# Transposing the last eight LayerNorm blocks on TensorE instead of by DMA, with new planner constants, in an attention and gMLP kernel

## The chip, the cores and the metric

One core of one Trainium2 chip runs the whole kernel in one launch. The metric is the device time in microseconds (us) of one execution; the median of three runs is given. A core has five engines that run side by side: TensorE (PE, with its weight loads shown as PEld), VectorE (DVE), ScalarE (ACT), GpSimd (POOL) and SyncE (SP), whose queue here issues every DMA.

## The reference, cut to what matters

```python
# S = 2048 tokens, D = 448, 16 heads of 28, W = 8 keys per query, 2 apart; Fh = 896
x  = A_x
h  = x + A(layernorm(x))          # A: sliding, dilated attention
h2 = h + B(layernorm(h))          # B: gMLP

def A(x):
    q, k, v = heads(x @ wqkv)
    # query s sees keys s, s-2, ..., s-14 (those >= 0)
    attn = softmax(where(mask, q . k * scale, -1e9))
    return concat_heads(attn @ v) @ wo

def B(x):
    z  = gelu(x @ w_in)
    z1 = z[..., :Fh]
    z2 = layernorm(z[..., Fh:])
    g  = w_sp @ z2 + b_sp         # w_sp is 2048 x 2048: mixes the tokens
    return (z1 * g) @ w_out
```

The neighbours are taken by a band matrix: scores of a query block against all keys of its reach are computed densely, `exp` is taken, and the result is multiplied by a 0/1 mask (band, and even distance).

## The kernel before, in words

The kernel isn't a nest of loops in the order of its work. It fills a graph with tasks (`G.add`, `dma`), and `Graph.schedule` then plans them: a task names the engines that may do it with a planned duration, what it reads and writes, the buffers it takes, and a rank `prio`. The planner steps through planned time. It looks for the engine that can start something first, takes among the tasks that could start there within a short window the one of lowest rank, and so fixes the order of each engine's instructions and, where there is a choice between VectorE and ScalarE, the engine. `Sched` puts in the semaphores, and each engine runs its list in order. The ranks are formulas over constants in the dictionary `P` (L133 to L135); `pos(m)` is m * 128 / 114, the attention block in which 128-token block m lies.

The stages, each as tasks of 128-token blocks m = 0 to 15 or attention blocks i = 0 to 17 of 114 queries:

- Load of x (L505), of all weights, and small setup on GpSimd. The attention mask `maskb` is made from GpSimd's band tables by five small VectorE steps (L492 to L496) with the rank `mc`. 24 matmuls on constants (L550) with the last rank fill TensorE while it is otherwise idle.
- LN1, `layernorm(m, 0, ...)`, rank `ln_s * pos(m) + ln_o`: statistics (L558, L560) on VectorE, the reciprocal root on GpSimd (`rstd_of`, L608, L610), normalising into a block of the ring `tring` of six (L563), and a copy of 64 pad columns (L567). Then the transpose into `xT`, which holds the features on the partitions. `xT` lies in the memory of `wsp0`, so the profile shows it as `wsp`; `wqk` and `wv` lie in `early`. For m < `nld` = 8 four TensorE transposes go to PSUM (L582) and VectorE or ScalarE copies them out (`copy_on`, L604 or L605). For m >= 8 four DMA transposes of 128 by 128 write `xT` directly (L590).
- `xU` is `xT` with its two partition halves exchanged, so that two matmuls of 64 rows can run side by side in the array. For m < `npt` = 8 copies on VectorE or ScalarE make it; for m >= 8 two DMAs per group of four blocks do (L600).
- Q and K, `qk_pair(tc, g, ...)`: for each group tc of 512 tokens four pairs of matmul chains (L619) and an eviction on ScalarE. It needs `xT` and `xU` of the four blocks of its group.
- Attention, `att_block(i)`: V (L627), scores (L660), `exp` in two parts (L669), mask product on VectorE (L676, rank `mk`), the weighted sum (L681), normalising (L686, L688), transpose back (L693).
- `y_block(m)`: output projection (L627), residual (L708), and LN2, `layernorm(m, 1, ...)`, whose transposes go to `xB` by DMA (L451); its exchanged copy `xS` is made by DMA too (L576).
- gMLP: z2 with its gelu (L743) and LayerNorm (L747 to L752), rank `z0 + zs * pos(m)`, its gelu placed behind the `exp` of attention block `zb`; z1 with its gelu (L769), rank from `z1`, behind the last `exp`. `load_wsp` fetches w_sp in four parts of 16 DMA transposes (L451) into `wsp0` (only once `xT` is dead) and `wsp1`. `g_tile(fc, tc)` is 16 matmuls of 512 columns (L777), the bias (L782) and the product with z1 (L785). `wout_block(m)` is the last projection (L795), the residual (L799) and the store (L801). The ranks of these lie between 60 and 100.

All DMAs stand in SyncE's one queue in the planned order, and a DMA whose data isn't ready holds up those behind it. A DMA transpose of LN1 is planned with 0.45 us of that queue (`P_TR_US`).

Of the kernel before, what the change touches and what calls it, by code (L numbers as in the profile page):

```python
# [15 lines left out]
NCH = 4  # L16
# [83 lines left out]
class Task:  # L100
# [3 lines left out]
    def __init__(self, idx, alts, fns, reads, writes, adds, allocs, prio, keep, table, mode, twos, dma_us):  # L104
# [22 lines left out]
WIN = {"pe": 0.15, "act": 0.05, "dve": 0.15, "pool": 0.05, "sp": 0.05}  # L127
DMA_US = 2.6
NSEM = 96
P_TR_US = 0.45  # L130


P = dict(ln_s=0.9, ln_o=-0.7, qk_s=2.2, qk_o=-11.38, qk_g=-2.74, v=14.25, ve=2.52, lg=-13.21, ex=-15.44, mk=-14.58, av=2.77,  # L133
         nm=0.59, ot=-4.62, y=12.08, ln2=5.39, z0=150.45, zs=-0.36, zb=13, kz2=2, z1=116.86, kl=1, kq=0, kz=5, switch=13.45,
         npt=8, nld=8, mc=25.81)  # L135


class Graph:
# [30 lines left out]
    def schedule(self):  # L169
# [14 lines left out]
        while ready:  # L184
# [37 lines left out]
            lim = first[eng] + WIN[eng]  # L222
            best = min((c for c in by_task.values() if c[3] == eng and c[0] <= lim), key=lambda c: (c[2].prio + (P["switch"] if c[3] == "pe" and c[2].mode != mode else 0.0), c[2].idx))
            s, e_at, t, eng, d = best
# [113 lines left out]
def bass_sequential_preLN__sliding_local_dilated__mixer_gmlp__prompt_kernel(  # L338
# [13 lines left out]
    G = Graph()  # L352

    with contextlib.ExitStack() as top:
        def sb(name, shape, dt):
            return top.enter_context(nc.sbuf_tensor(name, shape, dt))
# [3 lines left out]
        tring = sb("tring", [128, NTR, DP], BF16)  # L360
        xB = sb("xB", [128, NB, NCH, 128], BF16)
        xS = sb("xS", [128, NB, NCH, 128], BF16)
        ident = sb("ident", [128, 128], BF16)
# [35 lines left out]
        psb = psum[:].bitcast(BF16)  # L399
# [6 lines left out]
        r_ident, r_mask, r_bb, r_warm, r_ij, r_half, r_wout = [  # L406
            Res(n) for n in ("ident", "mask", "bb", "warm", "ij", "half", "w_out")]
# [17 lines left out]
        P_bank = Pool("bank", 8)  # L425
# [16 lines left out]
        def banks(b, i, n, p1=128):  # L442

            s = sorted(x.slot for x in b)
            return psum[:].rearrange("p (b c) -> p b c", c=512)[0:p1, s[i]:s[i + 1] + 1:s[i + 1] - s[i], 0:n]

        def dma(fn, kb, reads=(), writes=(), prio=0.0, after=(), adds=(), allocs=()):
            return G.add([("sp", 0.5)], [fn], reads, writes, adds=adds, allocs=allocs, prio=prio, after=after, dma_us=kb / 180.0)

        def dma_t(dst, src, us, reads=(), writes=(), prio=0.0, adds=()):  # L450
            return G.add([("sp", us)], [lambda e: e.dma_start(dst(), src(), transpose=True)], reads, writes, adds=adds, prio=prio)  # L451

        def pe_us(n, cols):
            return n * (cols / 2400.0 + 0.003)

        def act_us(n, sbuf=False):
            return (n + (190 if sbuf else 105)) / 1200.0

        def dve_us(n, rate=1.0):
            return (n / rate + 85) / 960.0  # L460
# [3 lines left out]
        def pos(m):  # L464
            return m * 128.0 / NQ
# [25 lines left out]
        for fn, rd, wr in (  # L491
# [5 lines left out]
        ):  # L497
            G.add([("dve", 0.28)], [fn], rd, wr, prio=P["mc"])

# [49 lines left out]
        for i in range(NWARM):  # L549
            G.add([("pe", 0.22 if i > 12 else 0.43)], [lambda e: e.matmul(bank(wb, 512), ident[:, :], warm)],  # L550
                  reads=[r_ident, r_warm], writes=[] if i else [wb], adds=[wb] if i else [], allocs=[] if i else [wb],
                  prio=900)

        def layernorm(m, i, prio):

            k = i * NB + m
            s = Buf(P_st)
            G.add([("dve", dve_us(D))], [lambda e: e.bn_stats(st[:, s.slot, 0:6], x_tm[:, m, :])],  # L558
                  [r_x[m]], [s], [s], prio=prio)
            G.add([("dve", 0.10)], [lambda e: e.bn_aggr(mv[:, k, :], st[:, s.slot, 0:6])], [s], [r_mv[k]], prio=prio)  # L560
            rstd_of(k, prio)
            t = Buf(P_tr)
            G.add([("dve", 0.32)], [lambda e: e.tensor_scalar(tring[:, t.slot, 0:D], x_tm[:, m, :], mv[:, k, 0:1],  # L563
                                                              rstd[:, k:k + 1], ALU.subtract, ALU.mult)],
                  [r_x[m], r_mv[k], r_rs[k]], [t], [t], prio=prio, after=tr_init)
            if not i:
                G.add([("dve", dve_us(64, 4)), ("pool", 0.25)], [lambda e: e.tensor_copy(tring[:, t.slot, D:], tring[:, t.slot, 384:D])],  # L567
                      [t], [t], prio=prio)
            xm = (xB[:, m, :, :] if i else xT[:, :, 128 * m:128 * m + 128])
            um = (None if i else xU[:, :, 128 * m:128 * m + 128])  # L570
            rm, ru = (r_xhT[m], r_xS[m]) if i else (r_xT[m], r_xU[m])
            if i:
                dma_t(lambda: xm, lambda: tring[:, t.slot, :], 1.3, [t], [rm], prio)
                if m % 2:
                    for dst, src in ((LO, HI), (HI, LO)):
                        dma(lambda e, dst=dst, src=src: e.dma_start(xS[dst, m - 1:m + 1, :, :], xB[src, m - 1:m + 1, :, :]), 131,  # L576
                            r_xhT[m - 1:m + 1], [], prio=prio, adds=r_xS[m - 1:m + 1])
                return
            if m < P["nld"]:
                b = Buf(P_bank)  # L580
                G.add([("pe", 0.27)], [
                    lambda e, c=c: e.transpose(psb[:, b.slot * 1024 + c * 128: b.slot * 1024 + c * 128 + 128],  # L582
                                               tring[:, t.slot, c * 128:(c + 1) * 128], ident[:, :]) for c in range(NCH)],
                    [t, r_ident], [b], [b], prio=prio)
                G.add([("act", act_us(512)), ("dve", dve_us(512, 2))], [
                    lambda e: copy_on(e, xm, psb[:, b.slot * 1024: b.slot * 1024 + 512].rearrange("p (c t) -> p c t", c=NCH))],
                    [b], [rm], prio=prio)
            else:
                for c in range(NCH):
                    G.add([("sp", P_TR_US)], [lambda e, c=c: e.dma_start(xm[:, c, :], tring[:, t.slot, 128 * c:128 * c + 128], transpose=True)],  # L590
                          [t], [], adds=[rm], prio=prio)
            if m < P["npt"]:
                for ps, po in ((LO, HI), (HI, LO)):
                    G.add([("dve", dve_us(384, 4)), ("act", act_us(384, True))], [
                        lambda e, ps=ps, po=po: copy_on(e, um[ps, 0:3, :], xm[po, 0:3, :])], [rm], [], adds=[ru], prio=prio)
            elif m % 4 == 3:
                cols = slice(128 * m - 384, 128 * m + 128)
                rms, rus = r_xT[m - 3:m + 1], r_xU[m - 3:m + 1]
                for dst, src in ((LO, HI), (HI, LO)):
                    dma(lambda e, dst=dst, src=src: e.dma_start(xU[dst, :, cols], xT[src, 0:3, cols]), 196, rms, [], prio=prio, adds=rus)  # L600

        def copy_on(e, dst, src):
            if hasattr(e, "activation"):
                return e.activation(dst, src, AF.Copy)  # L604
            return e.tensor_copy(dst, src)  # L605

        def rstd_of(k, prio):
            G.add([("pool", 0.24)], [lambda e: e.tensor_scalar(va[:, k:k + 1], mv[:, k, 1:2], EPS, None, ALU.add)],  # L608
                  [r_mv[k]], [r_va[k]], prio=prio - 20)
            G.add([("pool", 0.61)], [lambda e: e.tensor_tensor(rstd[:, k:k + 1], va[:, k:k + 1], mhalf[:, 0:1], ALU.pow)],  # L610
                  [r_va[k], r_half], [r_rs[k]], prio=prio - 20)
# [5 lines left out]
        def pair(b, ws, xs, n):  # L617

            return [lambda e, j=j, u=u: e.matmul(bank2(b, j, n), ws(j, (LO, HI)[j], u), xs(j, (LO, HI)[j], u), start=(u == 0),  # L619
                                                 stop=(u == 6), tile_position=(64 * j, 0)) for u in range(7) for j in range(2)]  # L620
# [5 lines left out]
        def full(b, ws, xs, n, m=128):  # L626
            return [lambda e, c=c: e.matmul(bank(b, n, 0, m), ws(ALL, c), xs(ALL, c), start=(c == 0), stop=(c == NCH - 1))  # L627
                    for c in range(NCH)]

        def pair_us(n):  # L630
            return pe_us(7, n)

        def qk_pair(tc, gg, prio):
# [3 lines left out]
            def src(j, ps, u):  # L637
                if u == 6 or u % 2 == j:
                    return xT[ps, u // 2, cols]
                return xU[ps, u // 2, cols]  # L640
            G.add([("pe", pair_us(512))], pair(b, lambda j, ps, u: wqk[ps, u, gg, :], src, 512),
                  r_wqk + r_xT[4 * tc:4 * tc + 4] + r_xU[4 * tc:4 * tc + 4], b, b, prio=prio, mode=1, twos=True, keep=P["kq"])
            G.add([("act", act_us(1024))],
                  [lambda e: copy_on(e, qk[:, :, gg, cols], banks(b, 0, 512))], b, [r_qT[tc][gg], r_kT[tc][gg]], prio=prio)

        def att_block(i):
            t0, nq, k0, nk = _att_geom(i)
            v, b = Buf(P_V), Buf(P_bank)
            G.add([("pe", pe_us(4, D))], full(b, lambda ps, c: xT[ps, c, k0:k0 + nk], lambda ps, c: wv[ps, c, :], D, nk),
                  r_xT[k0 // 128:(k0 + nk - 1) // 128 + 1] + r_stv, [b], [b, v], prio=i + P["v"], after=v_init)  # L650
            G.add([("act", act_us(D)), ("dve", dve_us(D))], [
# [82 lines left out]
        for m in range(NB):  # L734
            k = 2 * NB + m
            s = Buf(P_st)
            p = P["z0"] + P["zs"] * pos(m)
            zb = [Buf(P_bank), Buf(P_bank)]
# [4 lines left out]
                lambda e, zb=zb, m=m: e.activation(z2p[:, m, :].rearrange("p (b c) -> p b c", b=2), banks(zb, 0, D), AF.Gelu_apprx_tanh)],  # L743
# [124 lines left out]
```

## Time and profile before

| | |
|---|---|
| median of three runs | 284.14 us (284.07 to 284.81) |
| the profiled execution | 284.14 us, its span 282.4 us |
| TensorE (PE) busy | 246.5 us, 87% of the span |
| VectorE (DVE) busy | 155.7 us, 55% |
| ScalarE (ACT) busy | 100.8 us, 36% |
| GpSimd (POOL) busy | 49.9 us, 18% |
| mean granted TensorE clock | 0.958 |

The span runs from the first to the last instruction. A row of waits names the waiting engine and line, whom it waited for, the total in us, the number of times and the longest. A row of a timeline has the start, the length, the engine, line and operation, and the tiles. The chain that ended last is followed back from the last instruction through whatever released each step; "SPq" is SyncE's queue, "DMA" the transfer itself. Matmuls of one pair run at the same time, so their durations overlap.

### The profile page before, as it was taken

Reading aid. Unit: us, or ns where it says so; the run is one execution under the profiler, and the core shown is the slowest. Engines: PE = TensorE matmul, PEld = TensorE weight load, DVE = VectorE, ACT = ScalarE, POOL = GpSimd, SP = SyncE. Lnnn points to the kernel's source line nnn. Section 1 sums busy time; section 2 is a strip of 40 time slices with the busy share of each in tenths; the row PEclk is TensorE's granted clock in tenths of the full one; section 3 lists DMA queues with packets and bytes.
Section 4 is the critical chain, followed back from the end, with each engine's and each line's share of the span. In section 5 each row is a group of like instructions: output and inputs, shape, how many; then the busy total and the mean of one; then the engine's idle time right before and its main releaser. Section 6 shows DMA issues by size and latency. Waiting matters only on the chain.

```text
span 282.4 us, 5019 instructions
## 1 busy us (share of the span) xinstructions
PE 246.5 (87%) x2044; PEld 121.1 (43%) x2044; DVE 155.7 (55%) x354; ACT 100.8 (36%) x122; POOL 49.9 (18%) x125
## 2 busy tenths in 40 slices
PE   6996993049449999998799999999999999999994
PEld 2442462025215664544355444444444444444442
DVE  4968989204275899998798300753333333333333
ACT  2657787007409998996466600000000000000000
POOL 9442603200031021433443200000000000000000
PEclk9998899559959999999999999999999999999999
DMA  6990141131153405564555362444403442010001
GB/s 159 317 235 2 38 96 23 28 74 27 34 123 76 94 2 81 131 112 93 123 99 116 64 182 56 70 96 98 121 2 81 104 97 84 0 65 0 2 0 65
DMA packets 62806, 23.07 MB, mean 82 GB/s; under 512 B 53184, under 2 KB 61632, under 8 KB 62784
## 3 DMA queue, kind: packets, MB, share of 16 engines
q1 hardware_dynamic: 62784, 22.76, 35.5%
q8 instruction: 16, 0.26, 0.4%
q14 instruction: 6, 0.05, 0.1%
HBM read 6.49 MB, written 1.84 MB: 29 GB/s over the span
## 4 chain that ended last, share of the span: by engine, by line
PE 75%; DVE 8%; SPq 6%; DMA 3%; POOL 3%; ACT 2%; issue 2%; DVEq 0%; POOLq 0%
PE psum L777 34%; PE psum L619 22%; PE psum L795 7%; PE psum L627 7%; SPq L590 4%; DMA xU<-wsp 2%; PE psum L681 2%; SPq L451 2%; DVE z1p L676 2%; PE psum L660 1%; ACT z1p L669 1%; DVE st L747 1%; DVE tring L563 1%; DVE xU L605 1%; PE psum L693 1%
## 5 line engine op out<-in xcount | busy, mean ns | idle before, releaser
L782 DVE TENSOR_TENSOR qk<-psum,bb 128x512 bf16<-128x512 f32 x28 | 19.3, 690 | 68.8 <-PE psum L777 68.8
L777 PE MATMUL psum<-wsp,z2p 128*128 128x512 bf16 x224 | 48.9, 379 | 0.0
L777 PE MATMUL psum<-early,z2p 128*128 128x512 bf16 x224 | 48.8, 379 | 0.0
L619 PE MATMUL psum<-wsp,early 64*128 64x512 bf16 x128 | 29.3, 417 | 22.2 <-DMA xU<-wsp 22.2
L669 ACT ACTIVATE z1p<-psum 128x912 bf16<-128x912 f32 (+2 forms) x36 | 33.5, 934 | 1.7 <-PE psum L660 1.2
L604 ACT ACTIVATE qk<-psum 128x1024 bf16<-128x1024 f32 (+1 forms) x26 | 21.8, 841 | 33.4 <-PE psum L619 33.4
L777 PEld LDWEIGHTS psum<-wsp,z2p 128*128 128x128 bf16 x224 | 21.8, 98 | 26.6 <-issue 0.4
L777 PEld LDWEIGHTS psum<-early,z2p 128*128 128x128 bf16 x224 | 21.9, 98 | 26.3
L610 POOL TENSOR_TENSOR rstd<-va,mhalf 128x1 f32<-128x1 f32 x48 | 31.6, 658 | 3.7
L608 POOL TENSOR_SCALAR va<-mv 128x1 f32<-128x1 f32 x48 | 12.2, 254 | 95.6 <-DVE mv L560 77.2
L619 PE MATMUL psum<-xU,early 64*128 64x512 bf16 x96 | 27.1, 424 | 0.0
L619 PE MATMUL psum<-w,xB 64*128 64x448 bf16 x112 | 22.7, 350 | 2.8 <-DMA xS<-xB 1.5
L619 PEld LDWEIGHTS psum<-wsp,early 64*128 64x128 bf16 x128 | 11.3, 103 | 31.8 <-issue 25.2
L619 PE MATMUL psum<-w,xS 64*128 64x448 bf16 x112 | 22.7, 350 | 0.0
L795 PE MATMUL psum<-xS,z1p 128*128 128x448 bf16 x112 | 21.8, 353 | 0.0
L619 PE MATMUL psum<-xB,w 64*128 64x512 bf16 x98 | 21.8, 377 | 0.0
L619 PE MATMUL psum<-xS,w 64*128 64x512 bf16 x98 | 21.8, 377 | 0.0
L747 DVE BATCH_NORM_STATS2 st<-z2p 128x6 f32<-128x448 bf16 x32 | 19.4, 606 | 3.6 <-ACT z2p L743 3.3
L676 DVE TENSOR_TENSOR z1p<-z1p,maskb 128x1824 bf16<-128x1824 bf16 (+2 forms) x18 | 19.8, 1100 | 2.0 <-ACT z1p L669 1.8
L558 DVE BATCH_NORM_STATS2 st<-x_tm 128x6 f32<-128x448 bf16 x32 | 19.4, 605 | 1.6 <-DMA x_tm<-in_A_x_dram 1.5
L769 ACT ACTIVATE z1p<-psum 128x1024 bf16<-128x1024 f32 x14 | 14.3, 1023 | 8.5 <-PE psum L619 8.5
L563 DVE TENSOR_SCALAR tring<-x_tm,mv,rstd 128x448 bf16<-128x448 bf16 x32 | 12.3, 392 | 9.1 <-DMA xB<-tring 6.6
(69 smaller groups left out, 278.8 us busy)
## 6 DMA issues: line engine op xcount, KB each, us to landing
xS<-xB SPq DMA_DIRECT2D x16, 128.0 KB, 2.4
out_dram<-tring SPq DMA_DIRECT2D x16, 112.0 KB, 1.7
x_tm<-in_A_x_dram SPq DMA_DIRECT2D x1, 896.0 KB, 8.2
w<-in_B_w_in_dram SPq DMA_DIRECT2D x8, 112.0 KB, 3.3
early<-in_A_wqkv_dram SPq DMA_DIRECT2D x2, 392.0 KB, 5.5
w<-in_B_w_in_dram SPq DMA_DIRECT2D x2, 392.0 KB, 7.8
xS<-in_B_w_out_dram SPq DMA_DIRECT2D x1, 784.0 KB, 4.7
xU<-wsp SPq DMA_DIRECT2D x4, 192.0 KB, 2.9
```

Source lines behind the costliest of these rows:

```text
L558: G.add([("dve", dve_us(D))], [lambda e: e.bn_stats(st[:, s.slot, 0:6], x_tm[:, m, :])], [r_x[m]], [s], [s], prio=prio)
L563: G.add([("dve", 0.32)], [lambda e: e.tensor_scalar(tring[:, t.slot, 0:D], x_tm[:, m, :], mv[:, k, 0:1], rstd[:, k:k + 1], ALU.subtract, A ...
L604: return e.activation(dst, src, AF.Copy)
L610: G.add([("pool", 0.61)], [lambda e: e.tensor_tensor(rstd[:, k:k + 1], va[:, k:k + 1], mhalf[:, 0:1], ALU.pow)], [r_va[k], r_half], [r_rs[ ...
L619: return [lambda e, j=j, u=u: e.matmul(bank2(b, j, n), ws(j, (LO, HI)[j], u), xs(j, (LO, HI)[j], u), start=(u == 0), stop=(u == 6), tile_p ...
L627: return [lambda e, c=c: e.matmul(bank(b, n, 0, m), ws(ALL, c), xs(ALL, c), start=(c == 0), stop=(c == NCH - 1)) for c in range(NCH)]
L669: lambda e, hh=hh: e.activation(E[0:nk, ev.slot, hh * 4:hh * 4 + 8, 0:nq].rearrange("p (b g) q -> p b g q", b=2), banks(lb, hh, 512, nk).r ...
L676: lambda e: e.tensor_tensor(E[0:nk, ev.slot, :, 0:nq], E[0:nk, ev.slot, :, 0:nq], maskb[0:nk, mi:mi + 1, 0:nq].to_broadcast([nk, NHEAD, nq ...
L747: lambda e, h=h, m=m, s=s: e.bn_stats(st[:, s.slot, 6 * h:6 * h + 6], z2p[:, m, D * h:D * (h + 1)])],
L777: lambda e, s=s: e.matmul(bank(b, 512), z2p[:, s, fc * 128:(fc + 1) * 128], w[:, s, :], start=(s == 0), stop=(s == NB - 1)) for s in range ...
L782: G.add([("dve", dve_us(512))], [lambda e: e.tensor_tensor(ub[:, u.slot, :], bank(b, 512), bb[:, 512 * tc:512 * (tc + 1)], ALU.add)], [b, ...
L795: lambda e, f=f: e.matmul(bank(b, D), z1p[:, f, 128 * m:128 * m + 128], w_out[:, f, :], start=(f == 0), stop=(f == FC7 - 1)) for f in rang ...
```

## The change

LN1's path for blocks 8 to 15 becomes that of blocks 0 to 7: four TensorE transposes and one copy out of PSUM, in place of four DMA transposes. The constants `nld` and `P_TR_US` go. The exchange into `xU` for blocks 8 to 15 stays with the DMA. All the planner's constants in `P` but `kz2`, `kl` and `npt` get other values. The five mask steps and `wout_block` have the same text as before.

```diff
-P_TR_US = 0.45
...
-P = dict(ln_s=0.9, ln_o=-0.7, qk_s=2.2, qk_o=-11.38, qk_g=-2.74, v=14.25, ve=2.52, lg=-13.21, ex=-15.44, mk=-14.58, av=2.77,
-         nm=0.59, ot=-4.62, y=12.08, ln2=5.39, z0=150.45, zs=-0.36, zb=13, kz2=2, z1=116.86, kl=1, kq=0, kz=5, switch=13.45,
-         npt=8, nld=8, mc=25.81)
+P = dict(ln_s=0.13, ln_o=8.0, qk_s=2.85, qk_o=-21.56, qk_g=-2.68, v=11.96, ve=5.7, lg=-11.68, ex=-12.89, mk=-9.32, av=3.1,
+         nm=0.66, ot=-8.69, y=9.35, ln2=7.41, z0=63.24, zs=-1.6, zb=7, kz2=2, z1=109.63, kl=1, kq=1, kz=2, switch=7.46,
+         npt=8, mc=29.73)
...
-            if m < P["nld"]:
-                b = Buf(P_bank)
-                G.add([("pe", 0.27)], [
...
-            else:
-                for c in range(NCH):
-                    G.add([("sp", P_TR_US)], [lambda e, c=c: e.dma_start(xm[:, c, :], tring[:, t.slot, 128 * c:128 * c + 128], transpose=True)],
-                          [t], [], adds=[rm], prio=prio)
+            b = Buf(P_bank)
+            G.add([("pe", 0.27)], [
+                lambda e, c=c: e.transpose(psb[:, b.slot * 1024 + c * 128: b.slot * 1024 + c * 128 + 128],
+                                           tring[:, t.slot, c * 128:(c + 1) * 128], ident[:, :]) for c in range(NCH)],
+                [t, r_ident], [b], [b], prio=prio)
+            G.add([("act", act_us(512)), ("dve", dve_us(512, 2))], [
+                lambda e: copy_on(e, xm, psb[:, b.slot * 1024: b.slot * 1024 + 512].rearrange("p (c t) -> p c t", c=NCH))],
+                [b], [rm], prio=prio)
```

More of the change, by code (lines that the diff above doesn't have):

```diff
@@ L578, in layernorm @@
                 return
-            if m < P["nld"]:
-                b = Buf(P_bank)
-                G.add([("pe", 0.27)], [
[L582 to L587, printed above, removed]
-            else:
-                for c in range(NCH):
-                    G.add([("sp", P_TR_US)], [lambda e, c=c: e.dma_start(xm[:, c, :], tring[:, t.slot, 128 * c:128 * c + 128], transpose=True)],
-                          [t], [], adds=[rm], prio=prio)
+            b = Buf(P_bank)
[6 more added lines that the diff above has]
+                [b], [rm], prio=prio)
             if m < P["npt"]:
```

## The prediction

> **What bounds the kernel now.** I read the page's 40 slices first. In each row a digit is the busy tenths of a slice of 7.06 us.
>
> ```profile
> PE   6996993049449999998799999999999999999994
> DVE  4968989204275899998798300753333333333333
> PEclk9998899559959999999999999999999999999999
> ```
>
> TensorE is full from slice 20 (about 141 us) to the end. Before that there is a hole in slices 6 and 7 and a shallower one near slices 9 to 11, and VectorE is empty in the same places, so neither engine is the limit there. The waits say whom TensorE waits for (total us, times, longest):
>
> ```profile
> PE psum L619 <- DMA xU<-wsp: 22.2, 2, 14.3
> ```
>
> These are two waits of the Q/K projection (L619 in qk_pair) for the exchanged copy xU of tokens 1024 to 1535 and 1536 to 2047. The chain that ended last shows what stands before them (start, length, what):
>
> ```profile
> 53.27 1.23 SPq L590
> 54.55 1.23 SPq L590
> ...
> 56.33 0.63 SPq L600
> ...
> 57.02 2.91 DMA xU<-wsp
> 59.93 0.14 issue
> 60.06 6.62 PE psum L619 x42
> ...
> 160.86 24.28 PE psum L777 x112
> ```
>
> SyncE's queue issues one DMA transpose (L590) each 1.23 us, then the exchange (L600), and only then can TensorE go on. The same thing repeats up to 81.73. From 160.86 the chain is TensorE alone (L777, L795) to 278.73. The VectorE timeline shows that the data had long been there:
>
> ```profile
> 33.68 0.38 DVE L563 TENSOR_SCALAR tring<-x_tm,mv,rstd 128x448 bf16<-128x448 bf16 x1
> ...
> 49.05 0.39 DVE L563 TENSOR_SCALAR tring<-x_tm,mv,rstd 128x448 bf16<-128x448 bf16 x1
> ```
>
> Counting L563 and its pad copies L567 from the start, these are the normalised blocks 11 and 15, the last of the two groups. The exchanges start at 56.3 and 77.9, some 22 and 28 us later. That time is SyncE's queue.
>
> The windows answer prices the stages (PE busy, PEld, DVE, ACT, POOL, granted clock, DMA share, GB/s):
>
> ```profile
> 60.00:66.70 6.70, 6.64 (x50) 2.94 (x54) 0.00 (x0) 2.05 (x2) 0.00 (x0) 0.70 0.14 28
> 82.00:105.00 23.00, 22.90 (x322) 13.03 (x319) 18.28 (x37) 19.01 (x27) 4.60 (x11) 0.95 0.31 65
> 105.00:137.00 32.00, 28.96 (x352) 14.52 (x349) 29.25 (x67) 25.84 (x28) 10.10 (x24) 1.00 0.56 106
> ```
>
> After the hole the clock is 0.70, and three Q/K pairs take 6.62 us where a pair at full clock takes about 1.5 (four took 6.15 at 14.2). From 82 to 137 both TensorE and VectorE are nearly full.
>
> **The change part by part.** The diff holds two edits, the path of blocks 8 to 15 and the planner's constants. Nothing in it adds a mask step or alters wout_block, so I cost what the diff has.
>
> Removed: 32 DMA transposes at 1.23 us, 39.4 us of SyncE's queue between 27 and 76. Behind them now stand six loads of w1 (L530, held until 32.98), the exchanges L600 and the first LN2 transpose (L451 at 76.03), for which VectorE waited 6.6 us. The exchanges for blocks 8 to 15 stay: 0.6 us each to issue, 2.9 to land.
>
> Added: 8 times four TensorE transposes (L582). The chain has four at 0.34 to 0.40, so 2.7 us by the lower. Then 8 evictions of 128x512, 0.42 us on VectorE (3.4 in all) or 0.60 on ScalarE (4.8). TensorE is on the path, so its 2.7 counts in full. Evictions go to VectorE's sum below. New waits: TensorE's transposes stand in its order and can wait for a tring block; behind them wait projections and scores. The nearest row is TensorE waiting for L567 before L582, 2.0 us in three waits, 0.67 each: between 0 and 5.3 for eight. I take 0, since blocks 9 to 11 were ready within 3 us of each other.
>
> Where the stall goes: with block 11 normalised at 34.1, about 1 us for transpose and eviction and 3.5 us for the exchange, group 2 is ready near 39, before TensorE ran dry at 45.7. Group 3, from 49.5, is ready near 54. So both waits, 22.2 us, should go. Also the slow-clock stretches after them: 6.62 us against 4.6 for three pairs, and 4.52 against 3.1 for the two at 81.73, 3.5 us together.
>
> The Trainium skill speaks against this: "Advanced Engine Details and Errata", X-Bar Transpose (TRN2), says that transposing DMAs are as fast as plain ones, at 350 to 400 GB/s. As an estimate from that page, 32 transposes of 32 KB would take about 3 us of the queue, and the change would end near 281. The trace disagrees: a plain exchange of 192 KB holds the queue for 0.61 us, a transpose of 32 KB for 1.23, so the row decides.
>
> Sum against the profiled execution (284.14 us, span 282.4, 1.7 around it, equal to the median of the three runs): 284.14 - 22.2 - 3.5 + 2.7 = 261.1.
>
> What is late next is VectorE. It is busy 115.6 us before 160.86 (the ten-us windows added up); with the evictions, 119.0. The sum puts the spatial products (L777) at 160.86 - 23.0 = 137.9. From 82 to 137 VectorE was busy 47.5 of 55 us, 86%. At this pace from its first LayerNorm step at 2.9, 119.0 us of work ends at 141.3, 3.4 later. Not all of it must precede the products, and its pace in 20 to 46 was 22.8 of 26, 88%, so I add 2.9 and forecast 264.0.
>
> The constants: mask rank mc moves from 25.81 to 29.73. The five mask steps (L492 to L496, 1.2 us) ended at 14.05, and the first use (L676) was at 24.67; VectorE stood idle 1.93 us before 20.72. Cost 0 with that cover, 1.2 without. z0 falls from 150 to 63 and z1 stays near 110: w_in's second half (z2) now comes before its first (z1), and products g (60 to 100) come before z1. TensorE's sum is the same. z1 pairs among the products could cost something at each seam: TensorE shows no idle time from L619 to L777 at 160.86, so 0; the far end is 14 pairs at 0.42 us, the largest weight-load gap there, 5.9. I take 0, the nearer row. An order that also closes the other TensorE gaps (about 7 us between 7 and 137) could gain 3 or 4: 257 to 258. The w_sp transposes (L451, 1.26 us) start when the last V projection frees xT, at 105.6 now; they move with attention. The last 3.7 us after 278.73 stay.
>
> **The rivals.** *Part of the stall stays.* LN1's rank goes from 0.9 per block to a flat 8 to 10, so attention blocks rank ahead of it on VectorE and a group may be normalised late; the exchange, 3.5 us, is then exposed twice: 261.1 + 7 = 268; with half of the 22.2 kept it is 272, and with VectorE's 3.4 on top 275.6. For: VectorE was 88% busy from 20 to 46. Against: LN1 is what TensorE would starve for, and groups were ready 11 us before the dry point.
>
> *SyncE is the next limit.* From 105.6 to 172 it issues nearly without a pause; the 16th block of wsp0 is issued at 170, after the products have begun. If those loads move forward by only half of the 23 us, products start 11.5 us later than in the sum: 272.6. For: the queue was full there. Against: what fills it frees itself by the same 22 us.
>
> *Slower: table switches.* The gate zb falls from 13 to 7, so the gelu of z2 may run from attention block 7 on, between the exps of later blocks. Each round trip is two ACT_TABLE_LOADs of 1.28 us (ScalarE 108.40 to 109.69 shows no more): 2.57. The twelve exps of blocks 8 to 13 allow up to 12 more trips, 30.8 us. Nine uncovered trips eat the 23; ten give 261.1 + 25.7 = 286.8, all twelve 291.9. For: the trace already has two round trips. Against: ScalarE is busy 100.8 us in the first 161, with 4.8 more for evictions, so that most trips would be covered. The Trainium skill's "ScalarE: Activation LUTs", What ACT_TABLE_LOAD costs, adds a drain of about 1.38 us to each load. By that page the trip would be 5.3 and five trips would decide; the trace shows the next exp or gelu starting 0.01 us after the load.
>
> *The change does nothing*, because LN1 groups and exchanges are rearranged so that the same 22 us shows under another name: 283 to 285.
>
> **How the numbers follow.** Forecast (both waits gone, VectorE decides the rest) 0.70, with its own range 257 to 268. Part of the stall stays 0.14. SyncE 0.06. Table switches 0.08. Nothing 0.02. About 0.3%, 0.85 us, is what a measurement of this kernel can tell from no change. Faster 0.90, same 0.02, slower 0.08. The range runs from 257 (other gaps closed) to 276 (part of the stall with VectorE's lag); outside lie the slower case, the nothing case and a few hundredths below.
>
> **What would show it.** Right: no L590; 64 matmuls on the transpose line (L582 before) in place of 32; the row of TensorE waiting for xU under 5 us; slices 6 to 11 of PE at 8 or 9 and their clock at 0.9 or more; L777 starting near 138 to 142; VectorE at 85% or more from 20 to 140. Wrong: xU still above 10 us, group 2 of Q/K starting after 50 (part of the stall), ACT_TABLE_LOAD above 14 with TensorE waiting for L743 or L669 (switches), TensorE waiting for DMA wsp (SyncE), or a new row of over 10 us that none of these names.

## The result, and the profile after

The changed kernel takes 261.91 us (median of four runs, 261.79 to 263.56) against 284.15 for the kernel before in the same session. The ratio is 0.923, 95% interval 0.919 to 0.927: faster by 22.2 us. It lies in the range and near the sum of the prediction (261.1); the forecast itself, 264.0, was 2.1 too high. The profiled execution took 261.79 us, its span 260.1.

The 40 slices of the page of the changed kernel (a slice is now 6.5 us):

```profile
PE   6996999999999999699999999999999999999995
DVE  4997969998899999869970009423333333333333
PEclk9998699999999999999999999999999999999999
```

The hole in slices 6 and 7 and the shallow place at 9 to 11 are gone from both engines, and the clock stays at 9 from slice 5 on. One shallow slice is left in PE, slice 16, at 104 to 110 us. The largest wait of TensorE in the waits of this kernel, for xS, is there, in two pieces that end at 104.73 and 110.95; its row for xU is gone altogether:

```profile
PE psum L613 <- DMA xS<-xB: 3.0, 2, 1.9
```

L613 is the line that was L619. The timeline of SyncE's queue shows the two exchanges at 38 and 54 us, 18 and 24 us earlier than before:

```profile
38.20 1.28 SPq L594 DMA_DIRECT2D xU<-wsp  x2
...
53.58 1.25 SPq L594 DMA_DIRECT2D xU<-wsp  x2
```

The chain that ended last then runs through TensorE into the products:

```profile
128.52 10.38 PE psum L613 x98
138.90 24.28 PE psum L771 x112
```

138.90 stands against 160.86 before: nearly the whole gain, 22.0 of 22.3 us of span, is made ahead of the products, and the end is as it was. As a balance of TensorE: its busy time rose from 246.5 to 246.9 us, and its idle time fell from 282.4 - 246.5 = 35.9 to 260.1 - 246.9 = 13.2 us.

The windows of the stretches that were the hole (PE busy, PEld, DVE, ACT, POOL, granted clock, DMA share, GB/s):

```profile
46.00:60.00 14.00, 13.59 (x213) 7.40 (x209) 13.48 (x32) 11.15 (x14) 3.57 (x10) 1.00 0.18 40
82.00:105.00 23.00, 21.44 (x277) 11.21 (x276) 22.04 (x51) 18.20 (x21) 6.24 (x16) 1.00 0.47 93
```

VectorE is now busy 13.5 of 14 and 22.0 of 23 us: 95% and more, where the prediction had taken 86% for its pace.

### The profile page after: what moved, and what is told of

It is laid out like the page before. It is cut to its first block, busy times and chain, and to the rows that moved or that the text cites. A ratio compares the mean times of both kernels' runs of the same rounds, so it can differ in the third digit from the quotient of the medians.

```text
span 260.1 us, 5041 instructions
## 1 busy us (share of the span) xinstructions
PE 246.9 (95%) x2076; PEld 122.2 (47%) x2076; DVE 158.5 (61%) x362; ACT 97.5 (37%) x118; POOL 47.3 (18%) x127
## 4 chain that ended last, share of the span: by engine, by line
PE 87%; DVE 5%; POOL 3%; ACT 1%; DMA 1%; issue 1%; DVEq 0%; SPq 0%; POOLq 0%
PE psum L771 37%; PE psum L613 25%; PE psum L621 9%; PE psum L789 8%; PE psum L675 2%; PE psum L654 2%; PE psum L687 1%; DMA xS<-xB 1%; PE psum L580 1%; DVE xU L599 1%; DVE tring L562 1%; POOL rstd L604 1%; ACT qk L598 1%; ACT z1p L663 1%; PE psum L549 1%
## 5 line engine op out<-in xcount | busy, mean ns | idle before, releaser
L604 POOL TENSOR_TENSOR rstd<-va,mhalf 128x1 f32<-128x1 f32 x48 | 29.0, 606 | 3.4
L613 PE MATMUL psum<-wsp,early 64*128 64x512 bf16 x128 | 27.2, 395 | 0.1
L613 PE MATMUL psum<-w,xB 64*128 64x448 bf16 x112 | 22.8, 350 | 3.1 <-DMA xS<-xB 3.0
L602 POOL TENSOR_SCALAR va<-mv 128x1 f32<-128x1 f32 x48 | 11.6, 243 | 77.1 <-DVE mv L559 59.0
L613 PE MATMUL psum<-xU,early 64*128 64x512 bf16 x96 | 24.9, 396 | 0.0
L598 ACT ACTIVATE qk<-psum 128x1024 bf16<-128x1024 f32 (+1 forms) x21 | 19.1, 910 | 13.3 <-PE psum L613 11.8
L613 PE MATMUL psum<-w,xS 64*128 64x448 bf16 x112 | 22.9, 350 | 0.0
L613 PE MATMUL psum<-xS,w 64*128 64x512 bf16 x98 | 21.8, 376 | 0.0
L613 PE MATMUL psum<-xB,w 64*128 64x512 bf16 x98 | 21.8, 376 | 0.0
L737 ACT ACTIVATE z2p<-psum 128x896 bf16<-128x896 f32 x16 | 14.5, 916 | 9.7 <-PE psum L613 9.6
L621 PE MATMUL psum<-early,wsp 128*128 128x448 bf16 (+2 forms) x72 | 16.5, 353 | 0.1
```

## The experiments

**One part of the change alone.** The diff has two edits, so each was run without the other. Every ratio from here on is against the kernel before in the same session (its medians there are 285.43, 284.78 and 285.67 us). Theory Q: the stall is made by 32 slots of SyncE's queue at 1.23 us. Rival P: the new constants and the order they give bring the gain.

```diff
# path_only
-         npt=8, nld=8, mc=25.81)
+         npt=8, nld=16, mc=25.81)
```

> The kernel before with all 16 LN1 blocks transposed on TensorE, all its constants kept. Theory Q (the stall is made by the 32 queue slots of 1.23 us): the wait for xU falls from 22.2 us to under 5, time 261 to 268. Rival P (the new constants and their order bring the gain): the wait only changes its name, time 274 to 284.

Measured 269.21 us, ratio 0.947 (0.941 to 0.953). The wait for xU is gone and the products start at 138.5, so the queue was the cause. Yet 7 us are missing against the changed kernel. The end of its chain shows why:

```profile
235.14 1.64 PE psum L619 x14
236.80 4.43 DMA xS<-in_B_w_out_dram
241.27 22.66 PE psum L795 x111
```

One z1 pair (L619, 14 matmuls) ran after the last product. It has a worse rank (116.86 and up) than the products (60 to 100), and the planner came to it last. Its reading of xS keeps `w_out`, which lies in the same memory, from loading; so all of the last projection waits, 4.4 us with TensorE idle and a slower clock after it: its 111 matmuls (L795) take 22.66 us, where the chain of the kernel before has 21.02 for them in four pieces.

```diff
# const_only: all constants as in the diff of the change, but
-         npt=8, mc=29.73)
+         npt=8, nld=8, mc=29.73)
```

> The new constants with the DMA transposes of blocks 8 to 15 kept. Theory Q: the queue still issues 32 slots of 1.23 us ahead of the exchanges, TensorE waits for xU for 15 us or more, time 277 to 290. Rival P: the new order covers the queue, the wait is under 8 us, time 262 to 270.

Measured 290.13 us, ratio 1.018 (1.013 to 1.022): slower by 1 to 2%. TensorE waits 19.6 us for xU, in one piece, and here too one z1 pair is left to the end (4.6 us of waiting for `w_out`). The new order moves the stall and doesn't cover it. To take the left-over pair out, both were run again with one more constant changed:

```diff
# path_z1: path_only with
-z1=116.86
+z1=30
# const_z1: const_only with
-z1=109.63
+z1=50
```

> As path_only, with the rank of the z1 pairs at 30 instead of 116.86, so that none is left behind the products. Theory: what path_only lacked against the changed kernel (7.3 us) is mostly its last z1 pair, run at the very end, with w_out loaded only then (4.5 us of waiting and a slow clock after it): 261 to 265. Rival (the order of the first 137 us under the new constants carries it): 266 to 270.

> As const_only (new constants, DMA transposes kept), with the rank of z1 at 50 instead of 109.63, so that no pair is left behind the products. Theory Q: the wait for xU stays above 15 us; only the late pair's price goes: 281 to 286. Rival: without the late pair the new order covers the queue, 262 to 272.

path_z1: 262.12 us, ratio 0.922 (0.919 to 0.924), the changed kernel's time with the old constants but one. const_z1: 283.39 us, ratio 0.996 (0.993 to 0.998), a gain of 1.4 us, with the wait in place. The waits of const_z1:

```profile
PE psum L619 <- DMA xU<-wsp: 20.0, 1, 20.0
```

So the transposes carry the gain. The new constants alone bring at most these 1.4 us, and beside the transposes nothing that can be told apart; but they decide whether a z1 pair is left over, which costs about 7 us in these two pairs of runs.

**Half of the transposes.** Blocks 12 to 15 on TensorE, 8 to 11 still by DMA:

```diff
# group2_dma
-            if m < P["nld"]:
+            if m < P["nld"] or m >= 12:
```

> The kernel before, but only blocks 8 to 11 by DMA; 12 to 15 on TensorE. Theory Q: the first wait (14.3 us) stays, the second (7.9) goes with its slow clock (1.4), 1.4 us of TensorE transposes come in: 275 to 278. If the queue is not what holds group 3 (its LayerNorm is late instead): the second wait stays, 282 to 286.

Measured 289.53 us, ratio 1.016 (1.010 to 1.022): neither. The second wait for xU is gone, the first is 11.0 us, but a z1 pair was left over again (4.6), and TensorE now waits 7.5 us for w_sp. Without the left-over pair:

```diff
# group2_kz4: group2_dma with
-kz=5
+kz=4
```

> As group2_dma (8 to 11 by DMA, 12 to 15 on TensorE), kz 4 instead of 5, so that no z1 pair is left behind. Theory Q: one wait of 10 to 14 us for xU remains, the other stays away: 273 to 279. If the w_sp transposes (a wait of 7.5 us in group2_dma) decide instead: 280 to 285.

Measured 283.88 us, ratio 0.996 (0.994 to 0.999). That is the second branch: the 7.5 us for w_sp took the place of the second wait (7.9). To see whether this has to do with the transposes of LN1, blocks 8 to 11 got one DMA transpose each in the same order (group2_one, its edit is that of one_dma below):

> As group2_kz4 in the same order, with blocks 8 to 11 in one DMA transpose each instead of four. Theory Q: the remaining wait for xU (11.1 us) goes, with the slow clock after it; time 266 to 273, and the 7.5 us of waiting for w_sp stays or shrinks. Rival S (SyncE's w_sp loads set the time in this order): the wait for w_sp grows by what the other loses, time 279 to 284.

Measured 270.06 us, ratio 0.945 (0.941 to 0.949). The wait for xU went, as theory Q had it, and that for w_sp stayed, in the waits of group2_one:

```profile
PE psum L776 <- DMA wsp<-in_B_w_sp_dram: 7.4, 1, 7.4
```

In the same kernel's waits of SyncE's queue from 140 to 165 us, SyncE in its turn waits for TensorE:

```profile
SPq L451 <- PE psum L776: 5.6, 1, 5.6
```

In this plan's queue the first reload of `wsp0` (w_sp's third part), which must wait for the first products to have read it, stands ahead of the last two blocks of the first part, which those products still need. In the changed kernel's plan all 16 blocks of the first part stand ahead of the reload. This is the prediction's second rival, come true in another order. That order alone wasn't mended in a run, so this cause is read from the queue's order and the two waits.

**The planner told the true price.** It plans 0.45 us of queue for a transpose that takes 1.23.

```diff
# true_price (and kz=4 for kz=5)
-P_TR_US = 0.45
+P_TR_US = 1.23
```

> The kernel before with the planner told 1.23 us for a DMA transpose instead of 0.45 (and kz 4 for 5). Theory Q: 39 us of queue cannot be planned away, the wait for xU stays above 14 us, time 277 to 284. Rival M (the plan was misled by the price and could have covered the queue with other work): wait under 8 us, time 264 to 271.

Measured 289.42 us, ratio 1.016 (1.008 to 1.023). Both missed: TensorE's wait for xU shrank to 6.6 us, as the rival had it, and the time rose. The idle time of TensorE is 286.6 - 250.8 = 35.8 us, that of the kernel before (35.9), now spread over more waits:

```profile
PE psum L619 <- DMA xU<-wsp: 6.6, 1, 6.6
PE psum L777 <- DVE z2p L752: 6.3, 1, 6.3
PE psum L681 <- DVE z1p L676: 4.4, 7, 1.2
```

What was added is busy time, 250.8 us for 246.5, at a mean granted clock of 0.946 for 0.958. With these constants the queue time couldn't be planned away; whether other constants could is open.

**The price of a transpose.** Four transposes of 128 by 128 per block, or one of 128 by 512? Otherwise the instructions of every engine stand in the order of the kernel before.

```diff
# one_dma
-                for c in range(NCH):
-                    G.add([("sp", P_TR_US)], [lambda e, c=c: e.dma_start(xm[:, c, :], tring[:, t.slot, 128 * c:128 * c + 128], transpose=True)],
-                          [t], [], adds=[rm], prio=prio)
+                G.add([("sp", 4 * P_TR_US)], [lambda e: e.dma_start(xm, tring[:, t.slot, :], transpose=True)],
+                      [t], [], adds=[rm], prio=prio)
```

> The kernel before, old constants, blocks 8 to 15 still transposed by DMA, but each block in one DMA transpose of 128x512 instead of four of 128x128. Theory Q (the price is the queue slot of about 1.23 us per instruction): 8 slots, 10 us of queue in place of 39; the wait for xU falls under 5 us, and without TensorE's 2.7 us the time is 258 to 265. Rival T (the price goes with the data transposed): a slot of 4 us or more, the wait stays above 14 us, time 280 to 286.

Measured 261.02 us, ratio 0.916 (0.913 to 0.918). This is the cleanest of the runs: the old constants, DMA transposes, no work moved to another engine, and the whole gain. TensorE's wait for xU and the start of the products, then the line's own answer (durations in ns, min/median/max):

```profile
PE psum L618 <- DMA xU<-wsp: 0.7, 1, 0.7
...
138.19 24.28 PE psum L776 x112
...
L589 SPq DMA_TRANSPOSE wsp<-tring x8: 1189/1286/2343, 27.1 to 50.6; - x8
```

A transpose of four times the data holds the queue for 1.29 us, against 1.23. Between these two sizes the price goes with the instruction, not with the data: 32 slots of 1.23 us have become 8 of 1.29, about 29 us of queue less, and the stall is gone but for 0.7 us.

**VectorE's pace.** The prediction added 2.9 us for it. Here the mask product of the changed kernel is cut short, in the same order: 16 of the 114 columns of each block are masked, and the others left as they are.

```diff
# short_mask
-E[0:nk, ev.slot, :, 0:nq], E[0:nk, ev.slot, :, 0:nq], maskb[0:nk, mi:mi + 1, 0:nq].to_broadcast([nk, NHEAD, nq])
+E[0:nk, ev.slot, :, 0:16], E[0:nk, ev.slot, :, 0:16], maskb[0:nk, mi:mi + 1, 0:16].to_broadcast([nk, NHEAD, 16])
```

> The changed kernel with its order untouched, the mask product (L670) done on 16 of each block's 114 query columns; the other columns stay unmasked. VectorE's work falls by about 14 us before the products. Theory V (VectorE's pace sets when the products start, as the 2.9 us of the prediction had it): the products (138.90) start 5 us earlier or more, time 253 to 257. Rival T (TensorE's own work sets it, VectorE ends early enough): under 2 us of difference, time 259.5 to 262.5.

Measured 259.60 us, ratio 0.910 (0.905 to 0.916). VectorE's busy time fell from 158.5 to 144.5 us, and the products start at 137.36 in place of 138.90. 14 us less of its work bring 1.5 us by the profile and 2 to 3.5 by the times: that is rival T's branch. VectorE is felt, but doesn't set the pace; if it did, 14 us at the prediction's 86% would have brought about 16, as an estimate. The interval of the ratio doesn't meet that of the changed kernel (0.919 to 0.927), which was timed in the first session only, so "no difference" is unlikely too. The chains of the changed kernel and, behind the dots, of short_mask show where the 1.5 us are made:

```profile
24.62 1.56 POOL rstd L604
...
27.63 7.88 PE psum L613 x56
...
24.62 0.74 POOL rstd L604
...
26.59 7.86 PE psum L613 x56
...
137.36 10.74 PE psum L771 x49
```

1.0 of them stand ahead of the second group of Q/K, 26.59 in place of 27.63, and come by way of GpSimd: the reciprocal root (L604) that the next block waits for began with the first mask product (24.66, 1.09 us long in the changed kernel and 0.27 here), and in both runs ended about 0.4 us behind it. The 111 us from there to the products bring only 0.5.

**A better version.** The planner got durations nearer to the measured ones (L562 0.41 for 0.32, the rstd steps 0.32 and 0.64, L743 0.15, L746 0.44; 0.1 us of latency after a DMA, and 1.3 us for a transpose in best_one), and its constants were searched anew for the two ways of transposing.

```diff
# best_after: the changed kernel with these durations, and
-P = dict(ln_s=0.13, ln_o=8.0, qk_s=2.85, qk_o=-21.56, qk_g=-2.68, v=11.96, ve=5.7, lg=-11.68, ex=-12.89, mk=-9.32, av=3.1,
-         nm=0.66, ot=-8.69, y=9.35, ln2=7.41, z0=63.24, zs=-1.6, zb=7, kz2=2, z1=109.63, kl=1, kq=1, kz=2, switch=7.46,
-         npt=8, mc=29.73)
+P = dict(ln_s=0.17, ln_o=12.89, qk_s=1.96, qk_o=-14.66, qk_g=-3.17, v=8.64, ve=23.26, lg=-9.1, ex=-33.47, mk=-10.22, av=0.88,
+         nm=6.29, ot=-4.84, y=10.01, ln2=8.46, z0=52.71, zs=0.59, zb=4, kz2=0, z1=41.9, kl=1, kq=1, kz=0, switch=4.51,
+         npt=8, mc=40.58)
# best_one: one_dma with these durations, and
+P = dict(ln_s=0.84, ln_o=0.17, qk_s=1.93, qk_o=-12.74, qk_g=-2.05, v=8.37, ve=40.33, lg=-9.72, ex=-33.09, mk=-23.59, av=-2.91,
+         nm=-4.14, ot=-6.2, y=10.61, ln2=2.64, z0=66.61, zs=-4.81, zb=4, kz2=0, z1=117.86, kl=1, kq=1, kz=0, switch=9.52,
+         npt=8, nld=8, mc=48.43)
```

> One DMA transpose per block for 8 to 15 as in one_dma, the planner's durations set nearer to the measured ones, and its constants searched anew. One DMA takes 2.7 us from TensorE and a better order may close some of the 7 us of gaps before 137: 255 to 260. If the gaps are not the order's: 260 to 264.

> The changed kernel (TensorE transposes), the planner's durations set nearer to the measured ones, and its constants searched anew: 257 to 261 if the order closes gaps, 262 to 265 if it does not. It should stay 1 to 3 us behind the same search with one DMA per block.

best_one 259.58 us, ratio 0.908 (0.904 to 0.913); best_after 258.57 us, ratio 0.904 (0.900 to 0.910). Both beat the kernel before by 9% or more, and their intervals lie below that of the changed kernel (0.919 to 0.927). The expected lead of one DMA per block didn't show: the two can't be told apart. Which of the new durations and constants brings the gain over the changed kernel is open.

## Why the prediction was right

*The wait for xU, 22.2 us.* Right, and its cause too. path_only and path_z1 take it away by removing the slots, one_dma by merging them, const_z1 leaves it. The group's readiness was put a little early: the exchange of group 2 was issued at 38.20 and so landed near 42 rather than 39, that of group 3 near 57 rather than 54. The step had left out TensorE's own order. Blocks 9 to 11 were normalised by 32.9, but their transposes (L580) stand behind the four pairs of the group before:

```profile
27.63 7.88 PE psum L613 x56
35.53 1.03 ACT qk L598
36.70 0.83 PE psum L580 x12
```

TensorE had other work until 44.23 and about 58, so nothing came of it.

*The slow clock, 3.5 us.* Right for the stretches named: two pairs at 44.23 take 3.15 us and two at 56.51 take 3.13, full speed. What wasn't foreseen is that an earlier group became slower: the four pairs at 27.63 take 7.88 us at a clock of 0.78, before 7.0 at 0.88. The added transposes were busy 3.3 us (L580 6.1, L582 before 2.8) for the 2.7 of the sum, so the balance is 3.3 - 3.5 + 0.9 = 0.7. TensorE's busy time rose by 0.4, where the sum had it fall by 0.8; its idle time fell by 22.7, for 22.2.

*The new waits, taken as 0.* TensorE's waits for a tring block before its transposes (L580) are 2.0 us in all, the same as before. The wait for xS grew from 1.5 to 3.0, and that one had no term.

*VectorE, 2.9 us.* This is the term that failed. The step read VectorE's 86% in the full stretch before as the pace it can keep. But it was what TensorE's order asked of it. The windows of the changed kernel:

```profile
46.00:105.00 59.00, 57.03 (x814) 31.00 (x811) 55.89 (x124) 49.04 (x60) 13.78 (x35) 1.00 0.35 73
0.00:138.90 138.90, 128.88 (x1517) 67.63 (x1518) 118.37 (x290) 96.44 (x117) 47.27 (x127) 0.98 0.45 100
```

VectorE is busy 55.9 of 59 us from 46 to 105, 95%. Its work ahead of the products is 118.4 us, as the step counted it (119.0), and from 2.9 to 138.90 this makes 87%, about the share that the step used. So the share came out, and what failed is taking it for a limit: short_mask takes 14 us of the work away, and the start moves by 1.5. The products start at 138.90, nearer the sum's 137.9 than 141.3. Without the term the sum is 261.1, 0.8 below the measured median.

*The constants, 0.* Right as a sum: path_z1 has the changed kernel's time with the old constants but z1. The mask steps ended at 14.33 (14.05 before). But a term was missing that the runs priced: a z1 pair left behind the products costs about 6 to 7 us (269.21 to 262.12, 290.13 to 283.39, and 289.53 to 283.88). In the changed kernel no pair is left over, by the order its constants happen to give; that the sum came so near without this term is luck.

*The rivals.* No part of the stall stayed. The table loads of ScalarE fell from six to four instead of rising, so the gate `zb` = 7 cost nothing. As before, the next activation follows 0.01 us after a load (88.52 + 1.28 = 89.80, next at 89.81), and the one ahead of it ends at 88.50, so the drain of the page "ScalarE: Activation LUTs", What ACT_TABLE_LOAD costs, is again not seen in the row. SyncE didn't become the limit: the w_sp loads start at 84.24 in place of 105.60, and moved with attention by 21.4 us. group2_kz4 and group2_one, with 7.5 and 7.4 us of waiting for w_sp, show that the danger was real.

*The page that spoke against it.* "Advanced Engine Details and Errata", X-Bar Transpose (TRN2), of the Trainium skill has transposing DMAs as fast as plain ones. one_dma shows in what sense the row can be brought nearer to it: at 128 KB an instruction the slot is 1.29 us, at 32 KB 1.23. So small ones are dear; but a plain exchange of 192 KB holds the queue only 0.61 us, and no run here has a transpose as cheap as that.

## What to carry to other kernels

Where an engine waits for a DMA, look at what stands ahead of that DMA in its queue and count slots, not bytes: merging four small transposes into one was worth at least as much here as moving them to another engine. The busy share of an engine that isn't the bound tells what was asked of it and not what it can give, so a stage's next limit shouldn't be taken from it; taking work off that engine, as in short_mask, tells more. When an order is planned, a change of path or of constants can leave one piece of work to the end, which here cost 6 to 7 us; look for it before the two parts of a change are compared.

## What the runs showed of the hardware that was not expected

A DMA transpose of 128 by 512 elements (1.29 us, median of 8) holds the queue hardly longer than one of 128 by 128 (1.23 us, median of 32), while it moves four times as much. VectorE kept 95% busy for 59 us, and the time changed by about 1% when 14 us of its work were taken away. A reciprocal root on GpSimd that took 1.56 us beside a mask product of 1.09 us on VectorE took 0.74 beside one of 0.27 us; the median of the 48 is 0.57.
